# A new order of the start-up of chunked attention feeding a SoLU network, with some VectorE work given to GpSimd and two stores to SyncE

## The chip, the cores and the metric

The kernel runs on one core of a Trainium2 chip. A core has five engines with queues of their own: TensorE (PE) multiplies matrices, VectorE (DVE), ScalarE (ACT) and GpSimd (POOL) work elementwise, and SyncE (SP) issues transfers, which the core's 16 DMA engines carry out. The metric is the device time of one execution in microseconds (us); the time of a kernel is the median of several executions.

## The reference

Attention runs within chunks of 64 positions: 8 batches, 8 heads, 576 positions, head width 64. The heads are joined to 4608 rows of 512, and a network with a SoLU (h times softmax of h) and a normalization follows.

```python
scores = scale * np.matmul(q_c, k_c.transpose(0, 1, 2, 4, 3))
scores = scores - np.max(scores, axis=-1, keepdims=True)
attn = np.exp(scores)
attn = attn / (np.sum(attn, axis=-1, keepdims=True) + 1e-09)
out = np.matmul(attn, v_c)
...
h = x @ w_in                                  # 512 -> 1024
h_max = np.max(h, axis=-1, keepdims=True)
e = np.exp(h - h_max)
sm = e / (np.sum(e, axis=-1, keepdims=True) + 1e-09)
solu = h * sm
...
ln = (solu - mu) / np.sqrt(var + 1e-06) * g_ln
return (ln @ w_out).astype(np.float32)        # 1024 -> 512
```

## The kernel before, in words

The 4608 rows are cut into 36 tiles of 128 rows, two chunks each. For every tile the kernel turns q and k so that the head width lies on partitions, multiplies them to scores, takes the softmax, multiplies with v, multiplies the 512 columns with the first weight, applies SoLU and the normalization, turns the result z and multiplies it with the second weight. To keep accuracy each operand of the two large products is split into a high and a low part (x_h and x_l, wi_h and wi_l, z_h and z_l, wo_h and wo_l), and three of the four products of parts are added in PSUM: 24 products of 128x512 for each weight and tile.

The weights arrive as 64-bit numbers. Eight units of 1 MB (four of the first weight, four of the second) are loaded and put together from their two 32-bit words in steps.

The work falls into two parts. A loop over tiles 5 to 35 is the steady part. Ahead of it stands a start-up, written out as a list of words, START: each word calls one step of one tile or unit, and a word that comes again resumes a step that is in parts. Every engine takes its instructions in the order of this list, through a helper (the reason why nearly all instructions carry line 54). Only what is issued through `nc.scalar` directly is left to the scheduler, and that was the transfer of the first stores (line 630). A second list, MOVED, names steps that go to another engine than usual. The words, with what each part does and on which engine:

- `n:i`, `v:i`, `P:u`, `g`, `Q`/`q`: SP issues loads: q and k of tile i for turning on PE, v of tile i, weight unit u, the gain, a batch's q and k (32 transfers, eight for each `q:8`).
- `w:n`: n products of the identity with itself on PE, whose result nobody reads (the warm-up, line 717 on).
- `N:i:x`: four transpositions of q (x = 0) or k (x = 1) of tile i on PE; then their copy from PSUM on ACT, or on DVE if MOVED says so. `G`: the gain, turned.
- `S:i`: 32 small products for the scores. `A:i`: maximum and subtraction on DVE; then the exponential on ACT. `B:i`: sum, reciprocal and scaling on DVE (`softmax_b`). `T:i`: transposition of the probabilities on PE; then four copies on ACT. `U:i`: the same by a DVE transposition and, for odd i, eight transfers, four each from POOL and SP. `V:i`: 32 small products with v; x_h on ACT; x_l on DVE.
- `c:u`: clamp of unit u's upper words, on POOL; then a Prelu on ACT. `b:u`: the lower words, on DVE. `C:u`: the two joined, on DVE. `t:u`: high part, on ACT. `d:u`: low part, on DVE (`unit_low`).
- `M:i`: 24 products with the first weight (for tile 0 in four parts, one for each unit). `X:i`: row maximum on DVE; then the exponential on ACT. `Y:i`: a product and sum on DVE, the last reader of M's PSUM tile; then a linear step on ACT, or where MOVED puts it. `R:i`: the normalization's factor, on ACT and POOL.
- `z:i:x`: half x of z turned on PE; its copy z_h on ACT; z_l on DVE. `Z:i`: z turned on DVE and, for odd i, sixteen transfers, half from POOL, half from SP. `F`: a third of a tile's products with the second weight (eight). `o:i`: the result scaled on ACT and its store.
- `K:9`: q and k of tile 9 turned on DVE from batch 2's 32 loads.

There are two PSUM banks for transpositions, so a third group waits for the first one's copy. All tiles but tile 1 share one PSUM tile for M, so M of a tile waits for the first half of Y of the tile before. The first pass of the loop works on tile 5: it begins with M of tile 5, and eight microseconds later multiplies tile 2's z, which `Z:3` sent on its way, with the second weight.

Of the kernel before, what the change touches and what calls it, by code (L numbers as in the profile page):

```python
# [15 lines left out]


START = """
n:0 w:3 N:0:0 N:0:0 w:1 N:0:1 N:0:1 g w:1 S:0 A:0 G P:0 P:0 n:1 A:0 c:0 c:0 w:3 N:1:0 N:1:0 w:1
N:1:1 b:0 N:1:1 G P:1 w:1 S:1 B:0 v:0 C:0 A:1 t:0 T:0 T:0 c:1 c:1 w:4 V:0 V:0 P:2 b:1 c:2 n:2  # L20
d:0 P:3 A:1 n:3 w:6 N:2:0 w:1 N:2:1 C:1 V:0 B:1 t:1 c:2 T:1 N:2:0 b:2 N:2:1 T:1 d:1 S:2 n:4
M:0 M:0 C:2 t:2 c:3 c:3 v:1 A:2 A:2 b:3 d:2 C:3 N:3:0 N:3:1 N:3:1 M:0 N:3:0 S:3 N:4:0 B:2 N:4:1
t:3 N:4:0 A:3 P:5 d:3 c:5 N:4:1 A:3 T:2 T:2 S:4 V:1 M:0 P:4 n:5 B:3 T:3 V:1 V:1 M:1 X:0 X:0 T:3
A:4 A:4 b:4 v:2 N:5:1 c:4 n:6 P:7 c:5 N:5:0 c:4 Y:0 Y:0 n:7 N:5:1 V:2 b:5 v:3 B:4 N:5:0 V:2 b:7
C:4 z:0:1 P:6 v:5 N:6:0 X:1 v:4 C:5 N:6:0 S:5 Q:2 q:8 t:4 V:2 d:4 N:6:1 N:6:1 X:1 t:5 A:5 Y:1
M:2 z:0:1 z:0:1 X:2 A:5 R:0 z:0:0 z:0:0 q:8 N:7:1 q:8 c:6 S:6 Y:1 V:3 X:2 T:4 T:4 z:0:0 d:5 F
V:3 Y:2 Y:2 N:7:0 A:6 c:6 c:7 V:3 b:6 B:5 C:6 n:8 N:7:0 M:3 R:1 c:7 q:8 N:7:1 C:7 T:5 z:1:0 t:6
T:5 S:7 t:7 d:6 X:3 X:3 d:7 V:4 V:4 Y:3 Y:3 R:2 z:1:1 A:6 F F A:7 V:4 z:1:0 z:1:0 v:6 Z:2 A:7
M:4 F B:7 Z:3 o:0 V:5 z:1:1 z:1:1 B:6 F F v:7 X:4 N:8:0 X:4 U:6 U:7 V:5 Y:4 V:5 K:9 Y:4 N:8:0
R:4 R:3 N:8:1 N:8:1 o:1  # L30
"""
# [31 lines left out]
def chunk_attention_then_solu_ffn(  # L63
# [18 lines left out]
    G = S // 32  # L82
    NT = B * S // P
# [23 lines left out]
    def po():  # L107
# [26 lines left out]
    ident = const.tile([P, P], F32, name="ident")  # L134
# [93 lines left out]
    def unit_low(x):  # L228
        kind, m = UNITS[x]
        a, top = scaled.pop(x), tops.pop(x)  # L230
        if kind == "in":
            dve.tensor_tensor(
                out=paired(wi_l[:, m, :]),
                in0=a.rearrange("p h (a b x) -> p (h a) x b", b=P, x=2),
                in1=top.bitcast(F32), op=ALU.subtract,
            )
            return
        for y in range(2):
            dve.scalar_tensor_tensor(
                out=wo_l[:, 2 * m + y, :], in0=a[:, y],  # L240
                scalar=g_sb[:, 2 * m + y:2 * m + y + 1], in1=top[:, y].bitcast(F32),
                op0=ALU.mult, op1=ALU.subtract,
            )
# [132 lines left out]
    def softmax_b(i):  # L376
        e = st[i, "e"]
        ssum = small.tile([P, H], F32, name="s_sum")
        dve.tensor_reduce(out=ssum, in_=ES[i % 2], axis=AX.X, op=ALU.add)
        rinv = small.tile([P, H], F32, name="s_rinv")  # L380
        dve.reciprocal(out=rinv, in_=ssum)
        a = st[i, "e"] = work.tile([P, H, CH], F32, name="s_e") if i < PE_TURNED else e
        dve.tensor_tensor(
            out=a, in0=e, in1=rinv.unsqueeze(2).to_broadcast([P, H, CH]), op=ALU.mult,
        )

# [228 lines left out]
    def store(i):  # L615
        _, r = st.pop((i, "n"))
        o = work.tile([P, DM], F32, name="o_sb")
        sums = st.pop((i, "o"))
        for x, po in enumerate(sums):
            cols = slice(x * DM // len(sums), (x + 1) * DM // len(sums))  # L620
            act.activation(o[:, cols], po[:, cols], AF.Copy, scale=r)
            stores.append((out[i * P:(i + 1) * P, cols], o[:, cols]))
        if not order.on or i >= NT - 3:
            store_rest()

    stores = []

    def store_rest():
        for to, of in stores:
            (sync if order.on and len(stores) == 1 else nc.scalar).dma_start(to, of)  # L630
# [46 lines left out]
    def third():  # L677
        m, p = queue.pop(0)
        ffn_out(m, p, 3)
        if p == 2:  # L680
            store(m)

    def third_ahead():

        m, p = queue.pop(0)
        ffn_out(m, p, 3)
        if p == 1 and m + 1 < NT:
            whole(z_half(m + 1, 0))
        if p == 2:
            if m + 1 < NT:  # L690
                whole(z_half(m + 1, 1))
            store(m)
# [41 lines left out]
    begun = {}
# [15 lines left out]
    for i in range(first, NT):  # L750
# [99 lines left out]
```

## Time and profile before

| What | Value |
|---|---|
| median of 3 runs | 475.97 us (475.63 to 477.59) |
| the profiled execution | 477.95 us |
| its span, first to last instruction | 476.2 us |
| busy share of the span: PE, DVE, ACT, POOL | 98%, 79%, 54%, 31% |
| first product of the loop (M of tile 5) | 82.15 us after the span's start |

In the rows of the profile `out<-in` names the tiles that an instruction writes and reads: `ph` is M's PSUM tile, `po` F's, `sx` that of scores and values, `tp` the banks of transpositions, `h_nmax` is X's maximum, `z<-ph,z` Y's first half, `s_nmax` and `e<-sx` are A, `s_sum`, `s_rinv` and `e<-e,s_rinv` are B, `w_a` and `w_b` are units on their way, `nat` is q and k for turning, `q_st` and `k_st` a batch's q and k. Rows of a timeline give start, duration, engine, line, operation, tiles and, in brackets, the idle time before it and what ended it. An engine's successive rows overlap by some 0.08 us, so the time that a queue takes is read from start to start.

### The profile page before, as it was taken

To read this page: it belongs to the slowest core of one execution; us is meant where nothing else is said; L and a number is where in the kernel's file an instruction comes from. 1 tells how busy PE (TensorE), PEld (TensorE's weight loads), DVE (VectorE), ACT (ScalarE), POOL (GpSimd) and SP (SyncE) were. 2 spreads that over 40 slices of the span, in tenths; PEclk is the share of its full clock that TensorE was granted. 3 is DMA by queue.
4 is the path that set the end of the run, shared out by engine and by line. 5 is a ranking of instruction groups with operands and counts; after the bars stand their busy time and mean duration, and the time that the engine had idled before them with its cause. 6 is when DMAs were issued, how large, how long until landed. Compare 5 with 4: busy or idle time off the path is not lost.

```text
span 476.2 us, 11114 instructions
## 1 busy us (share of the span) xinstructions
PE 465.6 (98%) x4212; PEld 382.6 (80%) x4212; DVE 374.3 (79%) x520; ACT 256.5 (54%) x423; POOL 147.7 (31%) x298
## 2 busy tenths in 40 slices
PE   7899998999999999999999999999999999999997
PEld 5677786888888888888888888888888888888876
DVE  3999997798869887878787878797979797954441
ACT  2879982646444645454545455454555554545552
POOL 2212725150505050505050505032414141423330
PEclk9999999999999999999999999999999999999999
DMA  8999979758886878696358596949743435343221
GB/s 221 308 288 220 202 134 199 166 154 154 200 144 162 158 175 166 164 168 154 88 138 159 136 185 144 182 110 188 156 115 97 126 90 135 85 116 104 74 60 73
DMA packets 192924, 72.57 MB, mean 152 GB/s; under 512 B 177188, under 2 KB 177960, under 8 KB 191976
## 3 DMA queue, kind: packets, MB, share of 16 engines
q1 hardware_dynamic: 185768, 58.23, 55.4%
q0 software_dynamic: 6528, 12.86, 10.4%
q8 instruction: 33, 0.54, 0.5%
q10 hardware_dynamic: 576, 0.79, 0.5%
q14 instruction: 19, 0.16, 0.1%
HBM read 36.70 MB, written 9.44 MB: 97 GB/s over the span
## 4 chain that ended last, share of the span: by engine, by line
PE 85%; DMA 6%; SPq 3%; DVE 3%; ACT 1%; issue 1%; ACTq 0%
PE po L54 38%; PE ph L54 38%; PE tp L54 5%; PE sx L54 4%; SPq L54 3%; DMA nat<-in_k_dram 2%; DMA nat<-in_q_dram 2%; DMA z_t<-z_b 1%; DMA k_st<-in_k_dram 1%; DVE h_nmax L54 0%; DVE w_a L54 0%; DVE wo_l L54 0%; ACT attn_t L54 0%; ACT z L54 0%; ACT z_h L54 0%
## 5 line engine op out<-in xcount | busy, mean ns | idle before, releaser
L54 PE MATMUL ph<-wi_l,x_h 128*128 128x512 f32 x288 | 112.9, 392 | 1.9 <-DVE z L54 1.8
L54 PE MATMUL po<-wo_l,z_h 128*128 128x512 f32 (+1 forms) x288 | 113.3, 393 | 0.1
L54 ACT ACTIVATE z<-ph,h_nmax 128x1024 f32<-128x1024 f32 x36 | 40.2, 1117 | 134.6 <-DVE h_nmax L54 134.6
L54 PE MATMUL ph<-wi_h,x_h 128*128 128x512 f32 x288 | 112.1, 389 | 0.0
L54 PE MATMUL po<-wo_h,z_l 128*128 128x512 f32 (+1 forms) x288 | 111.9, 389 | 0.0
L54 PE MATMUL po<-wo_h,z_h 128*128 128x512 f32 (+1 forms) x288 | 111.4, 387 | 0.0
L54 POOL DMA_DIRECT2D z_t<-z_b x144 | 71.7, 505 | 28.7 <-DVE z_b L54 24.5
L54 PE MATMUL ph<-wi_h,x_l 128*128 128x512 f32 x288 | 78.1, 390 | 0.0
L54 POOL TENSOR_TENSOR u<-ssq,eps 128x1 f32<-128x1 f32 x36 | 7.1, 198 | 212.1 <-ACT sq L54 211.9
L54 DVE TENSOR_REDUCE h_nmax<-ph 128x1 f32<-128x1024 f32 x36 | 44.0, 1221 | 30.2 <-PE ph L54 30.2
L54 PEld LDWEIGHTS ph<-wi_l,x_h 128*128 128x128 f32 x288 | 54.1, 188 | 13.8 <-ACT x_h L54 2.2
L54 PEld LDWEIGHTS po<-wo_h,z_l 128*128 128x128 f32 x288 | 54.1, 188 | 12.1 <-DVE z_l L54 1.0
L54 PEld LDWEIGHTS po<-wo_l,z_h 128*128 128x128 f32 x288 | 54.1, 188 | 11.9 <-ACT z_h L54 0.5
L54 PEld LDWEIGHTS ph<-wi_h,x_l 128*128 128x128 f32 x288 | 53.9, 188 | 11.6 <-DVE x_l L54 0.4
L54 PEld LDWEIGHTS ph<-wi_h,x_h 128*128 128x128 f32 x288 | 54.1, 188 | 11.0
L54 PEld LDWEIGHTS po<-wo_h,z_h 128*128 128x128 f32 x288 | 54.1, 188 | 10.5
L54 DVE TENSOR_TENSOR z_l<-z_t,z_h 128x1024 fp32r<-128x1024 f32 (+1 forms) x37 | 42.0, 1136 | 25.3 <-ACT z_h L54 23.9
L54 DVE SCALAR_TENSOR_TENSOR z<-ph,z 128x1024 f32<-128x1024 f32 x36 | 43.9, 1219 | 13.3 <-ACT z L54 13.2
L54 ACT ACTIVATE z<-z,z_sum 128x1024 f32<-128x1024 f32 x33 | 38.1, 1154 | 23.0 <-DVE z L54 22.4
L54 DVE STREAM_TRANSPOSE z_b<-z 128x1024 f32<-128x1024 f32 x34 | 41.2, 1211 | 3.8 <-ACT z L54 3.1
L54 ACT CAST z_h<-z_t 128x1024 fp32r<-128x1024 f32 (+1 forms) x37 | 35.9, 970 | 8.6 <-PE po L54 6.5
L54 ACT ACTIVATE o_sb<-po,r 128x512 f32<-128x512 f32 (+1 forms) x36 | 24.2, 673 | 24.9 <-POOL r L54 18.6
(76 smaller groups left out, 598.6 us busy)
## 6 DMA issues: line engine op xcount, KB each, us to landing
out_dram<-o_sb SPq DMA_DIRECT2D x33, 256.0 KB, 2.5
v_sb<-in_v_dram SPq DMA_DIRECT2D x32, 256.0 KB, 4.4
z_t<-z_b POOLq DMA_DIRECT2D x128, 64.0 KB, 2.8
z_t<-z_b SPq DMA_DIRECT2D x128, 64.0 KB, 2.9
q_st<-in_q_dram SPq DMA_DIRECT2D x96, 72.0 KB, 3.1
k_st<-in_k_dram SPq DMA_DIRECT2D x96, 72.0 KB, 3.1
w_raw<-in_moe_w_out_dram SPq DMA_DIRECT2D x4, 1024.0 KB, 7.4
attn_t<-a_b POOLq DMA_DIRECT2D x60, 64.0 KB, 3.8
```

Of the source, the lines that this page charges most:

```text
L54: ins = make(*args, **kwargs)
```

## The change

- START has the same words in another order, except for the warm-up: 21 products become 9, and each is 512 columns wide instead of 256. Unit 1 is loaded first, ahead of q and k of tile 0. M:0 starts after N:3, S:3 and N:4:0, where it used to start after S:2. X:3 is followed by d:6, Z:2, d:7, A:7 and only then by Y:3; it was followed by d:7 and Y:3. K:9 stands ahead of Y:4 instead of behind it, and U:7 ahead of Z:3.
- MOVED gives to GpSimd the scalings of B:0 and B:2 to B:7 and the low words d:0, d:2 and d:3. It gives to DVE the copies N:3:0, N:5:0, z:1:0 and z:1:1 (before on ACT) and Y:4's linear step (ACT); N:0:0 and N:8:0 go from DVE to ACT, b:7 from GpSimd to DVE, the linear steps of Y:0 and Y:3 from GpSimd to ACT.
- The stores of tiles 0 and 1 used to be issued by `o` on ScalarE's queue, outside the order. Now `o` only notes them, and two new words, O:0 and O:1 near the end of the list, issue them from SP.

```diff
-R:4 R:3 N:8:1 N:8:1 o:1
+P:1 n:0 b:1 w:3 N:0:1 c:1 c:1 P:0 n:1 C:1 P:0 g N:0:1 t:1 N:0:0 N:0:0 c:0 P:2 w:2 S:0 N:1:1
+N:1:1 d:1 N:1:0 c:2 c:0 A:0 A:0 n:2 N:1:0 G c:2 G b:0 C:0 w:2 S:1 v:0 N:2:0 B:0 N:2:0 A:1 t:0
+A:1 n:3 N:2:1 N:2:1 b:2 T:0 T:0 w:1 S:2 C:2 d:0 N:3:0 A:2 A:2 B:1 w:1 V:0 N:3:0 P:3 c:3 N:3:1
+V:0 V:0 T:1 t:2 d:2 b:3 n:4 N:3:1 n:5 S:3 A:3 T:1 N:4:0 N:4:0 c:3 A:3 B:2 C:3 M:0 v:1 N:4:1
+N:4:1 M:0 t:3 v:2 P:5 P:4 d:3 B:3 N:5:0 N:5:0 N:5:1 V:1 V:1 c:5 T:2 n:6 M:0 T:2 M:0 V:1 N:5:1
+X:0 X:0 S:4 V:2 V:2 n:7 P:6 A:4 c:5 b:5 c:4 T:3 T:3 Y:0 v:3 V:2 C:5 b:4 M:1 A:4 Y:0 t:5 z:0:0
+z:0:0 B:4 N:6:0 M:2 R:0 X:1 c:4 z:0:0 d:5 X:1 C:4 N:6:0 P:7 t:4 N:6:1 Y:1 N:6:1 N:7:1 X:2 S:5
+c:6 c:7 V:3 c:6 N:7:1 V:3 d:4 Q:2 q:8 z:0:1 v:5 v:4 X:2 A:5 z:0:1 V:3 N:7:0 N:7:0 q:8 A:5 F c:7
+Y:1 Y:2 Y:2 S:6 T:4 T:4 M:3 b:7 z:0:1 B:5 b:6 T:5 A:6 z:1:0 A:6 C:6 C:7 X:3 R:2 S:7 V:4 t:6 t:7
+n:8 d:6 V:4 Z:2 d:7 T:5 A:7 X:3 Y:3 A:7 q:8 F F z:1:1 V:4 B:7 v:6 M:4 o:0 z:1:0 z:1:0 B:6 z:1:1
+q:8 z:1:1 Y:3 V:5 v:7 X:4 R:1 U:6 U:7 Z:3 V:5 V:5 F F X:4 K:9 Y:4 Y:4 N:8:1 F R:4 N:8:0 O:0
+N:8:0 N:8:1 o:1 R:3 O:1
...
-            dve.tensor_tensor(
+            (pool if f"d:{x}" in moved else dve).tensor_tensor(
                 out=paired(wi_l[:, m, :]),
...
-        dve.tensor_tensor(
+        (pool if f"B:{i}" in moved else dve).tensor_tensor(
             out=a, in0=e, in1=rinv.unsqueeze(2).to_broadcast([P, H, CH]), op=ALU.mult,
         )
...
-        if not order.on or i >= NT - 3:
+        if i >= NT - 3:
             store_rest()
...
+    def store_one(i):
+        sync.dma_start(*stores.pop(0))
...
-        m = ident.unsqueeze(1).to_broadcast([P, 2, P])
+        m = ident.unsqueeze(1).to_broadcast([P, 4, P])
```

The end of the old list, for comparison of the places named above:

```
A:4 A:4 b:4 v:2 N:5:1 c:4 n:6 P:7 c:5 N:5:0 c:4 Y:0 Y:0 n:7 N:5:1 V:2 b:5 v:3 B:4 N:5:0 V:2 b:7
C:4 z:0:1 P:6 v:5 N:6:0 X:1 v:4 C:5 N:6:0 S:5 Q:2 q:8 t:4 V:2 d:4 N:6:1 N:6:1 X:1 t:5 A:5 Y:1
M:2 z:0:1 z:0:1 X:2 A:5 R:0 z:0:0 z:0:0 q:8 N:7:1 q:8 c:6 S:6 Y:1 V:3 X:2 T:4 T:4 z:0:0 d:5 F
V:3 Y:2 Y:2 N:7:0 A:6 c:6 c:7 V:3 b:6 B:5 C:6 n:8 N:7:0 M:3 R:1 c:7 q:8 N:7:1 C:7 T:5 z:1:0 t:6
T:5 S:7 t:7 d:6 X:3 X:3 d:7 V:4 V:4 Y:3 Y:3 R:2 z:1:1 A:6 F F A:7 V:4 z:1:0 z:1:0 v:6 Z:2 A:7
M:4 F B:7 Z:3 o:0 V:5 z:1:1 z:1:1 B:6 F F v:7 X:4 N:8:0 X:4 U:6 U:7 V:5 Y:4 V:5 K:9 Y:4 N:8:0
R:4 R:3 N:8:1 N:8:1 o:1
```

More of the change, by code (lines that the diff above doesn't have):

```diff
@@ L18 @@
 START = """
[L19 to L29, printed above, removed]
-R:4 R:3 N:8:1 N:8:1 o:1
+P:1 n:0 b:1 w:3 N:0:1 c:1 c:1 P:0 n:1 C:1 P:0 g N:0:1 t:1 N:0:0 N:0:0 c:0 P:2 w:2 S:0 N:1:1
@@ L31 @@
+c:6 c:7 V:3 c:6 N:7:1 V:3 d:4 Q:2 q:8 z:0:1 v:5 v:4 X:2 A:5 z:0:1 V:3 N:7:0 N:7:0 q:8 A:5 F c:7
[3 more added lines that the diff above has]
+N:8:0 N:8:1 o:1 R:3 O:1
 """
 MOVED = """
-N:0:0=dve N:8:0=dve N:8:1=dve Y:0=pool Y:1=pool Y:3=pool b:7=pool c:0=pool c:1=pool c:2=pool
@@ L36 @@
-c:3=pool c:4=pool c:5=pool c:6=pool c:7=pool
+B:0=pool B:2=pool B:3=pool B:4=pool B:5=pool B:6=pool B:7=pool N:3:0=dve N:5:0=dve N:8:1=dve
+Y:1=pool Y:4=dve c:0=pool c:1=pool c:2=pool c:3=pool c:4=pool c:5=pool c:6=pool c:7=pool
+d:0=pool d:2=pool d:3=pool z:1:0=dve z:1:1=dve
 """
@@ L629, in store_rest @@
         for to, of in stores:
-            (sync if order.on and len(stores) == 1 else nc.scalar).dma_start(to, of)
+            (sync if len(stores) == 1 else nc.scalar).dma_start(to, of)
         stores.clear()
+    def store_one(i):
+        sync.dma_start(*stores.pop(0))
     NAT = -(-S // P)
@@ L721, in warm @@
             pe.matmul(
-                ph[:, 0, :2 * P].rearrange("p (x m) -> p x m", x=2), ident, m, start=True, stop=True
+                ph[:, 0, :].rearrange("p (x m) -> p x m", x=4), ident, m, start=True, stop=True
             )
@@ L730, in chunk_attention_then_solu_ffn @@
         "b": unit_bits, "C": unit_join, "t": unit_high, "d": unit_low, "M": ffn_in, "X": solu_a, "Y": solu_b,
-        "R": variance, "Z": z_turn, "z": z_half, "F": product, "o": store,
+        "R": variance, "Z": z_turn, "z": z_half, "F": product, "o": store, "O": store_one,
         "K": turn, "w": warm,
```

## The prediction

> **What bounds the kernel now.** I read the page's span first, then the busy time by stretch, with cuts where TensorE starts the products of row tiles 0, 2, 4 and 5 with the first weight (words M:0, M:2, M:4, and the first pass of the loop).
>
> ```profile
> span 476.2 us, 11114 instructions
> ```
>
> ```profile
> 0.00:23.36 23.36, 19.15 (x204) 14.58 (x205) 14.69 (x21) 13.14 (x20) 5.15 (x13) 1.00 0.93 264
> 23.36:44.41 21.05, 20.21 (x259) 16.06 (x253) 20.67 (x29) 17.00 (x30) 4.83 (x4) 1.00 1.04 253
> 44.41:67.24 22.83, 22.65 (x232) 18.43 (x230) 21.57 (x32) 21.73 (x43) 10.39 (x9) 1.00 0.89 184
> 67.24:82.15 14.91, 13.07 (x90) 10.12 (x88) 11.88 (x19) 4.66 (x10) 6.76 (x13) 1.00 0.99 186
> 82.15:476.20 394.05, 390.53 (x3440) 323.38 (x3440) 305.46 (x423) 200.00 (x324) 120.57 (x261) 1.00 0.61 137
> ```
>
> Columns: stretch, its length, then PE, weight loads, DVE, ACT, POOL busy, granted clock, DMA share, GB/s. From 82.15 on PE is busy 390.53 of 394.05 us, in code that the change leaves alone except for the place of two stores. So the change is worth what it moves the first product of the loop, now at 82.15. Call that point E. Ahead of it three things are nearly full at once: PE, DVE (20.67 of 21.05, 21.57 of 22.83) and the DMA engines (share 0.89 to 1.04). Relief on one of them only reaches the next.
>
> What ends last just ahead of E is in the chain of waits:
>
> ```profile
> 70.86 4.09 DMA k_st<-in_k_dram
> ...
> 75.03 0.41 ACTq L630
> ...
> 75.49 0.60 ACT z_h L54
> ...
> 76.11 0.69 DVE z_l L54
> ...
> 82.15 5.68 PE ph L54 x24
> ```
>
> The store of tile 0 (L630, on ScalarE's queue) waits for a k load, the copy z_h stands behind it, and DVE's z_l behind that. PE's own rows:
>
> ```profile
> 1.43 2.93 PE L54 MATMUL ph<-ident 128*128 128x256 f32 x6 [1.43 <-POOL e L357]
> ...
> 7.97 1.56 PE L54 MATMUL ph<-ident 128*128 128x256 f32 x6
> ...
> 49.08 1.07 PE L54 MATMUL ph<-wi_h,x_l 128*128 128x512 f32 x4
> ...
> 67.24 0.39 PE L54 MATMUL ph<-wi_l,x_h 128*128 128x512 f32 x1
> ...
> 72.71 0.39 PE L54 MATMUL po<-wo_l,z_h 128*128 128x512 f32 x1
> ...
> 79.27 1.04 PE L54 MATMUL tp<-ident,nat 128*128 128x128 f32 x8
> 82.15 0.47 PE L54 MATMUL ph<-wi_l,x_h 128*128 128x512 f32 x1 [1.84 <-DVE z L54]
> ...
> 90.19 0.50 PE L54 MATMUL po<-wo_l,z_h 128*128 128x512 f32 x1
> ```
>
> A tile's 24 products take 67.24 to 72.71, 5.47 us, so eight of them (a word F) 1.82; four transpositions (N, T, z) take half of 1.04, 0.52; I take 0.6 for the 32 small products of S or V. PE stands idle 1.84 us before E. So without the stall E comes at 80.3 at the earliest: 1.84 us, 0.4% of the span, is what moving the store can give in the old order of words. Under 0.5% is about what a measurement of this kernel can't tell from no change.
>
> **The change, step by step.** DVE's prices are best taken from start to start:
>
> ```profile
> 61.28 1.41 DVE L54 SCALAR_TENSOR_TENSOR wo_l<-w_a,g_sb,wo_h 128x512 fp32r<-128x512 f32 x2
> 62.60 1.22 DVE L54 TENSOR_REDUCE h_nmax<-ph 128x1 f32<-128x1024 f32 x1
> 63.78 1.41 DVE L54 SCALAR_TENSOR_TENSOR wo_l<-w_a,g_sb,wo_h 128x512 fp32r<-128x512 f32 x2
> ...
> 66.85 0.69 DVE L54 TENSOR_REDUCE s_nmax<-sx 128x8 f32<-128x512 f32 x1
> 67.58 0.69 DVE L54 TENSOR_TENSOR e<-sx,s_nmax 128x512 f32<-128x512 f32 x1
> 68.18 0.68 DVE L54 TENSOR_TENSOR x_l<-sx,x_h 128x512 fp32r<-128x512 f32 x1
> ...
> 69.38 1.24 DVE L54 STREAM_TRANSPOSE z_b<-z 128x1024 f32<-128x1024 f32 x1
> 70.54 0.65 DVE L54 TENSOR_REDUCE s_sum<-e 128x8 f32<-128x520 f32 x1
> ...
> 71.46 0.69 DVE L54 TENSOR_TENSOR e<-e,s_rinv 128x512 f32<-128x512 f32 x1
> 72.07 1.24 DVE L54 STREAM_TRANSPOSE z_b<-z 128x1024 f32<-128x1024 f32 x1
> ...
> 79.41 1.29 DVE L54 STREAM_TRANSPOSE a_b<-e 128x512 f32<-128x512 f32 x2
> 80.77 1.22 DVE L54 SCALAR_TENSOR_TENSOR z<-ph,z 128x1024 f32<-128x1024 f32 x1
> ...
> 82.52 0.70 DVE L54 STREAM_TRANSPOSE qT<-q_st 128x512 f32<-128x512 f32 x1
> ```
>
> That gives 1.32 for d of an output unit, 1.18 for X, 1.33 for A (66.85 to 68.18), 0.6 for x_l, sub of z, b or an eviction, all of 512 columns or at two a step (67.58 to 68.18), 1.16 for Z, 0.92 for the sum and reciprocal of B (70.54 to 71.46) and 0.61 for its scaling, 1.36 for U:6 and U:7 together, 1.2 for Y's first half (80.77's row), 1.2 for K:9 (twice 0.70, less the overlap); for C and d of an input unit, both over 1024 columns, I take X's 1.18.
>
> *Work moved.* DVE loses seven scalings (7 × 0.61 = 4.3) and three input units' low words (3 × 1.18 = 3.5), two evictions go and two come, and it gains b:7 (0.6), two evictions of z:1 (1.2) and the linear step Y:4 (bounded by 0.6 and 1.2). Net some 5 us less on DVE. This is off the path wherever DVE waits for PE.
>
> *Price on GpSimd.* No row has GpSimd on two wide inputs. Nearest are these, GpSimd's first and DVE's after them:
>
> ```profile
> 36.65 1.10 POOL L54 TENSOR_SCALAR w_a<-w_raw 128x1024 f32<-128x1024 f32 x1 [1.47 <-DMA w_raw<-in_moe_w_out_dram]
> 39.55 1.49 POOL L54 TENSOR_SCALAR z<-z,z_sum 128x1024 f32<-128x1024 f32 x1 [1.80 <-DVE z L54]
> 47.60 3.73 POOL L54 TENSOR_SCALAR w_b<-w_raw 128x1024 uint32<-128x1024 uint32 x1 [6.57 <-DVE s_nmax L54]
> ```
>
> ```profile
> 36.82 1.48 DVE L54 TENSOR_SCALAR w_b<-w_raw 128x1024 uint32<-128x1024 uint32 x1
> ```
>
> One input of 1024 columns takes 1.10, so a scaling of 512 lies between half of that, 0.55, and half of 3.73, 1.87. Two inputs at twice the one-input rate give 1.1, and 2.2 for a unit's low words; I take these. GpSimd gets 7 × 1.1 + 3 × 2.2 = 14.3 us and loses b:7 (3.73) and two linear steps (2.2), beside the 27 us that it is busy now ahead of E (5.15, 4.83, 10.39 and 6.76 of the stretches): no bound by itself. But the two engines get in each other's way: DVE's w_b began at 36.82 under GpSimd's w_a, which ended at 37.75, and took 1.48, so only 0.55 of it lies past that end; and GpSimd's z took 1.49 where w_a of the same size took 1.10. [...] Each moved operation can thus hand back to DVE between nothing and its own 1.1 or 2.2. Only those beside a DVE chain that sets PE's time count; there I take 0.5 in all, the overlap of B:5 with b:6, from 0 to 1.1.
>
> *Warm-up.* 21 products of 256 columns become 9 of 512. The first three cost 2.72 from 1.43 to the next row's start, later ones 0.52 each; twice that is 5.4 for the first three, then 1.04 each. They fill time in which PE waits for loads: unit 1 is now loaded ahead of tile 0's q and k, so the longer first group covers a later N:0. Taken as nothing.
>
> *To the end of M:2.* M:0 now stands behind N:3, S:3 and N:4:0, which PE used to do later (2.2 us). N:4:0 needs in all 6.5 MiB of loads (units 0 to 3, tiles 0 to 3 and half of 4, v:0), 6.8 MB. By 23.36 the trace had moved 0.264 × 23.36 = 6.2 MB; the rest at 253 GB/s takes 2.5, so 25.9, then N:4:0, its predecessors' evictions and M:0: I take 27.2 (26.4 if all is ready, 29 if the evictions queue on ACT behind unit 3's steps), against 23.36. From there to M:2 PE has M:0 and M:1 (10.9), seven groups of transpositions (3.6) and three of S or V (1.8): 16.3, and 0.5 for changes between them: M:2 at 44.0, its end at 49.5 to 49.8, against 50.15 now. The old list had also done N:6:1 and S:5 (1.1) by then. So the two orders are even here.
>
> *From the end of M:2 to M:4.* PE has three N, one of z and T:4 (2.6), S:5, S:6, V:3 (1.8), F (1.8), M:3 (5.5), then T:5 and z:1:0 (1.0), S:7 and V:4 (1.2), two F (3.6), z:1:1 (0.5): 18.0. DVE has in the new order X:2, d:4, A:5, x_l 3, Y:2 (5.6); b:7, a sub, B:5's sum, b:6, A:6, C:6, C:7 (6.4); X:3, d:6, Z:2, d:7, A:7, Y:3 (7.5): 19.5. M:4 writes the PSUM tile that Y:3 reads, so it waits for DVE: 49.7 + 19.5 + 0.2, and 0.5 of contention, M:4 at about 69.9, against 67.24. This is where the gain goes: X:3 waits for M:3, and four DVE steps stand between X:3 and Y:3 where the old list had one d.
>
> *From M:4 to E.* M:4 ends at 75.4. PE then has V:5, three F, two N, as now: 72.71 to the end of 79.27's row is 7.6, less 0.2 that the last one's pipeline hides: 7.4, so 82.8. DVE has X:4, U:6, U:7, Z:3, x_l 5, K:9, Y:4: 1.18 + 1.36 + 1.16 + 0.6 + 1.2 + 1.2 = 6.7, and 0.2: 82.3. The old stall behind the store is gone and DVE just fits beside PE, if K:9 does not wait.
>
> *K:9's wait.* K:9 reads batch 2's 32 loads of q and k. It used to stand behind Y:4; now Y:4 stands behind it.
>
> ```profile
> 70.13 6.02 SPq L54 DMA_DIRECT2D k_st<-in_k_dram x8
> ...
> 76.95 6.82 SPq L54 DMA_DIRECT2D z_t<-z_b x8
> ```
>
> ```profile
> L54 SPq DMA_DIRECT2D k_st<-in_k_dram x16: 443/496/1782, 64.1 to 75.6; - x16
> ...
> DMA to landing us min/median/max: 2.5/3.5/5.3
> ```
>
> The last two rows are the view of k_st: all 16 of its issues, shortest, median and longest, and their landing. SP issues its last one by 76.15, landed by 79.7 with the median and 81.4 with the longest. The new list has the same loads ahead, and v:6 as well (one issue more, 0.75). For E at 82.8 K:9 must start by 80.2. Landing at 79.0 to 81.5 thus costs 0 to 1.3; I take 0.
>
> *The stores and z_t.* O:0 and O:1 keep SP behind ACT's o:1, after U:7 and Z:3; nothing due early stands behind them. But SP now issues U:7's four copies (3.0 at k_st's 0.75 each) ahead of Z:3's eight (6.82). Z:3 leaves DVE some 3.2 us ahead of E (x_l 5, K:9, Y:4), U:7 4.3 ahead, so at these paces the last copy is issued 5.5 after E and lands 2.5 later; z_t's first user on PE comes 8.04 after E (90.19 less 82.15) and needs it split first, about 2.2. PE would wait 2. At 0.5 an issue, the median of k_st's 16, the last one is issued 1.7 after E and nothing waits. 0 to 2; I take 0.2, near the lower end, because SP's queue is empty by then.
>
> *Sum.* E goes from 82.15 to 82.8, and 0.2 come behind it: span 476.2 + 0.85 = 477.05. The profiled execution took 477.95, 1.75 over its span, so it would take 478.8; the median of the runs shown is 475.97, 1.98 below that execution, so the median becomes **476.8**.
>
> **The rivals.**
> *K:9 late (slower).* If the last k load lands past 80.2, E = landing + 2.6 (K:9, Y:4, 0.2). If the last eight start at 73 instead of 70.13, behind v:4, v:5 and v:6, take 6.02 for the issue and 5.3 to land, that is 84.3, E = 86.9 and the time 480.7. For it: DMA share 0.99 in the last stretch. Against: GpSimd's Z:3 copies no longer compete before that landing.
> *GpSimd in DVE's way (slower).* B:5, B:7 and B:6 stand beside DVE's 19.5 and 6.7; at 1.87 each and wholly in its way they add 5.6, half of it 2.8: E near 85.6, 479.4. It decides from 0.5 on, what I took. [...]
> *Only the store's stall goes (faster).* If DVE's four steps behind X:3 find time, because M:3 ends earlier than DVE's chain says or loads land without the pauses that they have now, PE alone sets E: 49.7 + 18.0 + 5.5 + 7.4 = 80.6, or 79.3 if M:0 starts at 26: 474.4 to 473.1. For it: 5 us less on DVE. Against: the sum of one queue in order, above.
> *Half clock (slower).* Ahead of M:0 PE has nine N, four S, two T, a V (9) and the warm-up (11.6), so it idles some 6.6 of its first 27.2 us, where the first stretch now leaves 4.2. In the trace the first six rows run at 0.45 each and later ones at 0.26. If it fell back to the first pace for half of M:0, 2.7 us of products take 4.7: 2.0 more, 478.6. [...]
> *The change doesn't do what it says.* Every step has its queue in the list, and the stores now have one too; under 0.01, and counted with the forecast.
>
> **How the numbers follow.** Forecast, E between 81.4 and 84.4 (475.4 to 478.4 with the 0.2): 0.62. PE alone sets E: 0.16, of which 0.09 goes under 473.6. K:9 late: 0.10. GpSimd: 0.08. Half clock: 0.04. The 0.5% bounds are 473.6 and 478.4. Faster: those 0.09 and 0.01 of the forecast's tail, 0.1. Slower: 0.08 of K:9, 0.06 of GpSimd, 0.03 of the clock, 0.17. The range takes in the faster rival down to 473.8 and the slower ones up to 479.4, and leaves 0.2 out.
>
> **What would show it.** Right: M:2 starts near 44; M:4 starts near 69.9, PE idle 1.5 to 2.5 us before it for DVE's z; PE idle little before E; ACT no longer idle for k loads near 75; GpSimd's scalings at 1.1 and low words at 2.2. Wrong: M:4 within 0.3 of PE's own pace, PE waiting on nat loads for more than 2 us between M:0 and M:1, E off by more than 1.5, or a change after E.

## The result, and the profile after

| | kernel before | changed kernel |
|---|---|---|
| median of its runs | 476.78 us (474.86 to 478.68, 6 runs) | 482.65 us (481.14 to 485.25, 6 runs) |
| the profiled execution, and its span | 477.95, 476.2 us | 481.58, 479.8 us |

The ratio is 1.0125 with a 95% interval of 1.0083 to 1.0167: 5.9 us slower, where 476.8 us in a range from 473.8 to 479.4 had been predicted. The profiled executions lie 3.6 apart only, because that of before is above its median and that of after below. Of the changed kernel's runs those granted a clock of 1.000 took 481.14 and 481.58 us, those at 0.992 and 0.993 took 484.88 and 485.25; the two between, at 0.995 and 0.999, took 482.12 and 483.19.

The busy time by stretch, cut at the first products of M:0, M:2, M:4 and E as in the prediction (stretch, length, PE, weight loads, DVE, ACT, POOL, clock, DMA share, GB/s):

```profile
0.00:29.23 29.23, 20.49 (x224) 11.47 (x225) 16.26 (x24) 16.28 (x26) 9.88 (x16) 1.00 1.04 251
29.23:46.72 17.49, 16.74 (x175) 13.45 (x174) 11.54 (x18) 12.64 (x22) 10.12 (x7) 1.00 1.00 281
46.72:72.58 25.86, 24.22 (x268) 19.26 (x266) 25.27 (x38) 23.35 (x45) 8.72 (x9) 1.00 0.89 172
72.58:85.31 12.73, 12.73 (x89) 10.30 (x89) 11.55 (x19) 4.44 (x9) 6.65 (x12) 1.00 0.68 129
85.31:479.80 394.49, 390.80 (x3443) 323.46 (x3440) 303.44 (x420) 199.50 (x323) 121.73 (x263) 1.00 0.61 137
```

E comes 3.16 us later than before (85.31 against 82.15), and 0.44 more is lost behind it. The late start is there at M:0 already: 29.23 against 23.36. PE idles 8.7 us of the first stretch, where it idled 4.2 of a shorter one. From M:2 on the stretches are near what was predicted: PE's one long wait is for Y:3 (1.11, the row at 72.58), and PE is never idle from M:4 to E.

```profile
28.85 0.63 PE L55 MATMUL tp<-ident,nat 128*128 128x128 f32 x4 [1.71 <-DMA nat<-in_q_dram]
29.23 0.48 PE L55 MATMUL ph<-wi_l,x_h 128*128 128x512 f32 x1
...
36.55 0.50 PE L55 MATMUL ph<-wi_l,x_h 128*128 128x512 f32 x1 [0.20 <-POOL wi_l L55]
...
72.58 0.50 PE L55 MATMUL ph<-wi_l,x_h 128*128 128x512 f32 x1 [1.11 <-DVE z L55]
```

Two things hold M:0. Its first part stands behind N:4:0, which waits for tile 4's q. Its last part needs unit 3's low words, and waits for them in spite of the late start. What unit 3 waited for is in the chain of waits (start, duration, what):

```profile
12.31 3.70 SPq L55
...
18.25 9.35 DMA w_raw<-in_moe_w_in_dram
...
27.75 1.53 POOL w_a L55
...
29.29 1.25 POOL wi_l L55
...
31.65 2.04 POOL s_e L55
...
34.07 2.44 POOL wi_l L55
...
36.55 1.65 PE ph L55 x6
```

The chain names one transfer and then GpSimd: the clamp, part of another unit's low words, a scaling, unit 3's low words. But the chain follows an engine's own queue where the waits are short, and the low words did not wait for the scaling, which ended at 33.69: their row (at 34.07, further down) has 0.38 of idle time that ScalarE's high part ended. ScalarE's rows give the other path:

```profile
29.57 0.59 ACT L55 COPY qT<-tp 128x512 f32<-128x512 f32 x1 [1.67 <-PE tp L55]
30.05 1.06 ACT L55 ACTIVATE w_a<-w_a 128x1024 f32<-128x1024 f32 x1
...
32.82 1.17 ACT L55 CAST wi_h<-w_a 128x1024 fp32r<-128x1024 f32 x1 [0.71 <-DVE w_a L55]
```

Unit 3's clamp ended at 29.28, its Prelu began at 30.05, behind the copy of N:4's q, which waited for PE; then come the join on DVE, the high part on ScalarE and the low words on GpSimd. The two paths end within 0.38 us of each other, so that is the most which a shorter path on ScalarE alone could gain, and a shorter queue on GpSimd alone gains nothing. In the trace of before, SP and GpSimd have for the same unit

```profile
14.06 4.85 SPq L54 DMA_DIRECT2D w_raw<-in_moe_w_in_dram  x1
```

```profile
24.14 1.13 POOL L54 TENSOR_SCALAR w_a<-w_raw 128x1024 f32<-128x1024 f32 x1 [4.62 <-DMA w_raw<-in_moe_w_in_dram]
```

so unit 3 has landed 3.6 us later in the new list, where tile 3's q and k are loaded ahead of it instead of behind. GpSimd's prices are near those taken, except under DVE's join:

```profile
17.55 1.04 POOL L55 TENSOR_TENSOR s_e<-e,s_rinv 128x512 f32<-128x512 f32 x1
...
31.65 2.04 POOL L55 TENSOR_TENSOR s_e<-e,s_rinv 128x512 f32<-128x512 f32 x1
34.07 2.42 POOL L55 TENSOR_TENSOR wi_l<-w_a,wi_h 128x1024 fp32r<-128x1024 f32 x1 [0.38 <-ACT wi_h L55]
```

```profile
31.15 1.64 DVE L55 SCALAR_TENSOR_TENSOR w_a<-w_a,w_b 128x1024 uint32<-128x1024 uint32 x1 [0.67 <-ACT w_a L55]
```

The scaling that began at 31.65, under DVE's join of two inputs (1.64, where the prediction takes 1.18 for it), took 2.04 instead of 1.04. The one at 17.55 took 1.04 beside DVE operations that read scores from PSUM. The join ended at 32.79 and the scaling 0.9 after that, so most of a scaling's 1.04 lies behind the join's end; by what the two hold each other up no row shows.

### The profile page after: what moved, and what is told of

Read it like the earlier page. It is cut to its first block, busy times and chain, and to the rows that moved or that the text cites. A ratio compares the mean times of both kernels' runs of the same rounds, so it can differ in the third digit from the quotient of the medians.

```text
span 479.8 us, 11071 instructions
## 1 busy us (share of the span) xinstructions
PE 465.0 (97%) x4188; PEld 377.9 (79%) x4188; DVE 368.0 (77%) x514; ACT 256.2 (53%) x422; POOL 157.1 (33%) x305
## 4 chain that ended last, share of the span: by engine, by line
PE 83%; DVE 5%; SPq 4%; DMA 3%; issue 2%; POOL 2%; ACT 1%; DVEq 0%; ACTq 0%; POOLq 0%
PE ph L55 38%; PE po L55 38%; SPq L55 4%; PE sx L55 4%; PE tp L55 4%; DMA w_raw<-in_moe_w_in_dram 2%; POOL wi_l L55 1%; DVE h_nmax L55 1%; DMA z_t<-z_b 1%; DVE wo_l L55 1%; DVE z L55 1%; DVE z_b L55 1%; DVE w_a L55 0%; DVE e L55 0%; POOL s_e L55 0%
## 5 line engine op out<-in xcount | busy, mean ns | idle before, releaser
L55 ACT ACTIVATE z<-z,z_sum 128x1024 f32<-128x1024 f32 x34 | 39.3, 1155 | 22.5 <-DVE z L55 21.9
L55 ACT ACTIVATE sq<-z 128x1024 bf16<-128x1024 f32 x36 | 37.5, 1043 | 4.5 <-DVE z L55 4.5
```

Of the source, the lines that this page charges most:

```text
L55: ins = make(*args, **kwargs)
```

## The experiments

Each ratio is against runs of the kernel before taken beside it, with its 95% interval; E, M:0, M:2 and M:4 are the starts of those products in the run's own trace.

**The parts of the change.** First the stores alone, in the old list:

```diff
-R:4 R:3 N:8:1 N:8:1 o:1
+R:4 R:3 N:8:1 N:8:1 O:0 o:1 O:1
```

> The old list and old engines; only the stores of tiles 0 and 1 go to SyncE, at the end of the list. If the stall behind the first store was worth what the rows say, PE's 1.84 us of idle time before the loop goes, the loop's first product comes at 80.3 to 80.6 instead of 82.15, and the kernel is 1.5 to 1.9 us (0.3 to 0.4%) faster than before. If another wait takes its place (DVE's chain up to Y:4, or loads), no change within 0.5 us.

Measured: 475.35 us, ratio 0.9974 (0.9957 to 0.999), E at 80.44, with no wait ahead of it:

```profile
79.65 1.03 PE L54 MATMUL tp<-ident,nat 128*128 128x128 f32 x8
80.44 0.48 PE L54 MATMUL ph<-wi_l,x_h 128*128 128x512 f32 x1
```

The stall is what the prediction read it as (80.3 without it), and this part alone is faster than both kernels. Next GpSimd's ten operations alone, in the old list:

```diff
+B:0=pool B:2=pool B:3=pool B:4=pool B:5=pool B:6=pool B:7=pool d:0=pool d:2=pool d:3=pool
```

> The old list; only the seven scalings of probabilities and the three low words go to GpSimd. If the new order is what costs, this is within 1 us of before, and the loop starts at 81 to 83. If GpSimd is what costs (its 1 us for a scaling and 2.4 us for low words in chains that PE waits for, and blocked turns beside DVE), this alone is 2 to 4 us slower than before.

Measured: 481.76 us, 1.0108 (1.0089 to 1.0127), E at 86.27. Rows of DVE, POOL, ACT and PE, and two stretches:

```profile
21.17 1.22 DVE L53 TENSOR_TENSOR wi_l<-w_a,wi_h 128x1024 fp32r<-128x1024 f32 x1
```

```profile
22.48 1.09 POOL L53 TENSOR_SCALAR w_a<-w_raw 128x1024 f32<-128x1024 f32 x1 [6.98 <-DVE wi_l L53]
23.53 2.40 POOL L53 TENSOR_TENSOR wi_l<-w_a,wi_h 128x1024 fp32r<-128x1024 f32 x1
```

```profile
23.60 1.06 ACT L53 ACTIVATE w_a<-w_a 128x1024 f32<-128x1024 f32 x1 [3.94 <-POOL w_a L53]
24.56 0.57 ACT L53 COPY qT<-tp 128x512 f32<-128x512 f32 x1
```

```profile
25.18 1.11 PE L53 MATMUL tp<-ident,s_e 128*128 128x128 f32 x4 [3.08 <-ACT qT L53]
```

```profile
20.00:25.00 5.00, 1.66 (x10) 1.11 (x10) 2.70 (x4) 1.40 (x2) 2.52 (x2) 1.00 1.09 309
25.00:30.00 5.00, 4.82 (x46) 3.88 (x47) 4.00 (x4) 4.18 (x9) 3.80 (x3) 0.66 1.30 206
```

Not GpSimd's busy time costs here: it stood idle for 6.98 us ahead of the clamp of unit 2 (the row at 22.48). What ended that wait was DVE's low words of unit 1, at 22.39. The moved operation, unit 0's low words, comes behind the clamp in GpSimd's queue (23.53). In the kernel before DVE had made them from 16.02 on, and the clamp of unit 2 began at 17.98, on the landing of its load. `w_a`, which a clamp writes and low words are the last to read, has two buffers (pool `work`); so the likely reading is that the move took away the buffer that used to come free first. It rests on these rows and the kernel's text; no run adds a buffer. The rest is shown by the rows: ACT's Prelu waits for the clamp, tile 2's copies stand behind the Prelu, and PE waits for the copies. Behind that idle of 3.08 us the granted clock is 0.66 over five microseconds. Then the reverse, the changed kernel with the ten operations back on DVE:

```diff
-B:0=pool B:2=pool B:3=pool B:4=pool B:5=pool B:6=pool B:7=pool d:0=pool d:2=pool d:3=pool
```

> The changed kernel with the same seven scalings and three low words back on DVE. If the order is what costs, the time stays within 1.5 us of the changed kernel (481 to 484), and the product of row tile 0 with unit 3 still starts after 35. If GpSimd is what costs, that product starts by 34, the loop by 83, and the time falls to 478 or less.

Measured: 489.21 us, 1.0261 (1.0235 to 1.0287), E at 90.64, with one wait of

```profile
37.20 0.66 PE L53 MATMUL tp<-ident,s_e 128*128 128x128 f32 x4 [3.11 <-DVE qT L53]
```

That is outside both ranges that were expected. So list and engines cannot be priced apart: the moves cost 5 us in the old list and save 6.6 in the new one.

**The clock.** The changed kernel with 17 wide warm-up products instead of 9, in the same places and two new ones ahead of T:1 and N:4:0:

```diff
-V:0 V:0 T:1 t:2 d:2 b:3 n:4 N:3:1 n:5 S:3 A:3 T:1 N:4:0 N:4:0
+V:0 V:0 w:1 T:1 t:2 d:2 b:3 n:4 N:3:1 n:5 S:3 A:3 T:1 w:2 N:4:0 N:4:0
```

> The changed kernel with 17 warm-up products of 512 columns instead of 9, the added ones where PE idled in the first 29 us. If the clock is the cause of what the median shows beyond the profiled run (the granted clock was 0.992 to 0.999 in four of the changed kernel's six runs, and those four were the longest), the clock is 1.0 in every run and the median falls by about 2 us, to 480 to 481. If the clock doesn't matter, the median stays at 482 to 483, or rises by what the added products delay.

Measured: 482.57 us, 1.0127 (1.0107 to 1.0146), clock 0.999 or 1.000 in all five runs, which lie within 1.1 us, but E at 86.38, because the products last past the load that they fill:

```profile
28.13 1.98 PE L55 MATMUL ph<-ident 128*128 128x512 f32 x4
29.95 0.60 PE L55 MATMUL tp<-ident,nat 128*128 128x128 f32 x4
```

They buy the steady clock with as much delay. The other way round, the kernel before with 9 of its 21 products (an excerpt; of the nine places five go, three keep two products each and the first keeps its three):

```diff
-N:0:0 w:1 N:0:1 N:0:1 g w:1 S:0 ... n:3 w:6 N:2:0 w:1 N:2:1
+N:0:0 N:0:1 N:0:1 g S:0 ... n:3 w:2 N:2:0 N:2:1
```

> The kernel before with 9 warm-up products of 256 columns in place of 21, nothing else changed. If the warm-up only fills time in which TensorE waits, E (first product of the loop) stays at 82.2 (81.9 to 82.5) and the time at 476.7. If idle time on TensorE lowers its clock, as in the rows of the run with only the GpSimd moves (clock 0.58 for 4 us after an idle of 3.08), some stretch of this run between 0 and 30 us shows a clock under 0.9, products there stand 0.4 apart instead of 0.23, E comes 1 to 2.5 us later and the time is 477.7 to 479.2.

Measured: 478.06 us, 1.0035 (1.0013 to 1.0057). Between 0 and 50 us the profiled run (clock 0.999) shows 1.00 throughout and M:0 2 us *earlier* (21.36), and E at 81.40; ten of the twelve runs were granted 0.989 to 0.996. But the lower ones among these are not the longer ones (476.92 us at 0.989, 480.71 at 0.993, 478.06 at 1.000). So neither expectation holds whole: less filling starts M:0 sooner, lowers the clock in most runs, and costs 0.35%, which the clock alone does not explain. In the profiled run PE still waits for Y:4 ahead of E (1.88), and the lead is lost behind E, in part in these two waits:

```profile
137.54 0.62 PE L54 MATMUL tp<-kT,qT 64*64 64x64 f32 x26 [0.27 <-DVE kT L54]
...
140.04 0.50 PE L54 MATMUL po<-wo_h,z_l 128*128 128x512 f32 x1 [0.69 <-DVE z_l L54]
```

**Y:3.** The changed kernel with X:3 and Y:3 ahead of A:7:

```diff
-n:8 d:6 V:4 Z:2 d:7 T:5 A:7 X:3 Y:3 A:7 q:8
+n:8 d:6 V:4 Z:2 d:7 T:5 X:3 Y:3 A:7 A:7 q:8
```

> The changed kernel with X:3 and Y:3 ahead of A:7's first half, nothing else changed. Step (M:2 to M:4) of the prediction: M:4 waits for Y:3 at the end of DVE's queue, 1.1 us of idle in the trace of the changed kernel. If so, M:4 comes 1.1 earlier after M:3 and E at about 84.2, the time near 481.5. The rival is that TensorE's own sequence or the next wait (z of tile 1, K:9) is as late: E 85.0 to 85.4, the time 482.6.

Measured: 481.67 us, 1.0115 (1.0074 to 1.0155). PE's wait ahead of M:4 falls from 1.11 to 0.23, as expected; the interval does not tell this kernel from the changed one. Its profiled execution was one with a clock of 0.993, and so shows what the changed front can do, since nothing ahead of M:3 differs:

```profile
25.00:30.00 5.00, 2.64 (x41) 2.22 (x42) 3.44 (x7) 2.99 (x7) 2.09 (x2) 0.78 0.97 153
30.00:35.00 5.00, 5.00 (x16) 3.99 (x15) 2.85 (x5) 3.56 (x5) 3.82 (x3) 0.54 1.03 265
```

```profile
28.71 1.08 PE L55 MATMUL tp<-ident,nat 128*128 128x128 f32 x4 [1.53 <-DMA nat<-in_q_dram]
29.45 0.78 PE L55 MATMUL ph<-wi_l,x_h 128*128 128x512 f32 x1
30.02 0.63 PE L55 MATMUL ph<-wi_h,x_h 128*128 128x512 f32 x1
30.45 0.63 PE L55 MATMUL ph<-wi_h,x_l 128*128 128x512 f32 x1
...
73.66 0.50 PE L55 MATMUL ph<-wi_l,x_h 128*128 128x512 f32 x1 [0.23 <-DVE z L55]
```

PE was busy 2.64 us of the five ahead of 30; the changed kernel's trace has 2.50 there and a clock of 1.00. Here the clock fell, M:0's products stood 0.43 apart (30.02 to 30.45), and M:2 came at 48.48 instead of 46.72: up to M:2 the half clock costs 1.8 us in this execution. The changed kernel's own runs at 0.992 and 0.993 took some 3.7 us longer than those at 1.000; how much of that is lost behind M:2 no trace shows. Nor does any show why it strikes some runs and not others: ahead of this fall no single wait is longer than 1.53 us (the row at 28.71), ahead of the fall to 0.66 above there is one of 3.08, and the changed kernel's own trace has one of 1.71 with the clock at 1.00 behind it.

**Inside the front.** M:0's first two parts ahead of N:4:

```diff
-T:1 N:4:0 N:4:0 c:3 A:3 B:2 C:3 M:0 v:1 N:4:1 N:4:1 M:0 t:3
+T:1 M:0 M:0 N:4:0 N:4:0 c:3 A:3 B:2 C:3 v:1 N:4:1 N:4:1 t:3
```

> The changed kernel with M:0's first two parts ahead of N:4 (they stood between N:4's two groups and behind them), nothing else changed. Theory one: the 1.71 us that TensorE waits for q of tile 4 in front of M:0 is what the new place of M:0 costs; then M:0 starts at 27.1 instead of 29.2, M:2 at 45.0, E at 83.6 and the time is 480.9. Theory two: M:0's last part waits for unit 3's low words, which GpSimd ends at 36.5; then M:0 starts at 27.1 too, but the fourth part still near 36.5, M:2 near 46.7, E near 85.3 and the time 482.6.

Measured: 484.17 us, 1.0177 (1.0134 to 1.0219). M:0 started at 27.42 and M:2 at 47.48, which is theory two. ACT's rows, and PE's:

```profile
30.97 0.59 ACT L55 COPY qT<-tp 128x512 f32<-128x512 f32 x1 [2.71 <-PE tp L55]
31.45 1.06 ACT L55 ACTIVATE w_a<-w_a 128x1024 f32<-128x1024 f32 x1
```

```profile
37.49 0.50 PE L55 MATMUL ph<-wi_l,x_h 128*128 128x512 f32 x1 [0.15 <-POOL wi_l L55]
```

Unit 3's Prelu now stood behind the copy of N:4, which waited for PE. Hence the next, with the Prelu ahead as well:

```diff
+T:1 c:3 M:0 M:0 N:4:0 N:4:0 A:3 B:2 C:3 v:1 N:4:1 N:4:1 t:3
```

(The word's first part, the clamp, stands further ahead, so this one is the Prelu.)

> As the run with M:0 ahead of N:4 (M:0 at 27.4, M:2 at 47.5, E at 86.2), and with the clamp and the Prelu of unit 3 ahead of M:0 and N:4, nothing else. In that run ScalarE's Prelu of unit 3 began at 31.45, though GpSimd's clamp had ended at 27.3, because the copy of N:4's q stood ahead of it in ScalarE's queue and waited for TensorE (idle 2.71). Theory (unit 3's chain through the queues sets M:0's last part): the Prelu starts near 28.4, the low words end near 34.0 instead of 37.4, M:2 starts at 44.3 to 45.3, E comes at 83.0 to 84.0, the time is 480.4 to 481.4. Rival (what the front lacks is loads and GpSimd time, not the order of queues): M:2 at 46.5 or later, E from 85.2 on, the time 482.6 or more.

Measured: 481.92 us, 1.0112 (1.0095 to 1.013); the Prelu began at 28.25, M:0's last part at 36.09 still behind GpSimd's low words, M:2 at 46.08, E at 84.82. Against the run before that is 1.4 earlier, as the theory has it, but not the 2.2 to 3.2 expected; against the changed kernel 0.5. The queue was one link of several: GpSimd stood idle for 1.23 us ahead of the low words (33.60), because ScalarE's high part began at 32.37, behind N:4's copies, though the join had ended at 31.48. With M:0 ahead of N:4, unit 3 loaded ahead of tile 3's q and k, and its low words on DVE (without the earlier Prelu):

```diff
-A:1 n:3 N:2:1 ... N:3:0 P:3 c:3 N:3:1
+A:1 P:3 n:3 N:2:1 ... N:3:0 c:3 N:3:1
...
-d:0=pool d:2=pool d:3=pool
+d:0=pool d:2=pool
```

> As the run before, and with unit 3's load ahead of tile 3's q and k and unit 3's low words on DVE instead of GpSimd. Theory two (unit 3 late): unit 3 lands 2 to 3 us earlier (24.6 to 25.6 instead of 27.6), M:0's fourth part no longer waits, M:2 starts at 44.0 to 45.0, E at 82.6 to 83.6, the time is 480.0 to 481.0. Theory one alone (only the wait for tile 4): no better than the run before. A third possibility: tile 3's q and k come later by as much, TensorE waits for N:3 instead, and E stays at 85.0 to 85.6.

Measured: 490.43 us, 1.029 (1.0252 to 1.0328). The third possibility, and worse than put (E at 91.75):

```profile
24.38 0.63 PE L55 MATMUL tp<-ident,nat 128*128 128x128 f32 x4 [2.35 <-DMA nat<-in_q_dram]
...
39.70 0.63 PE L55 MATMUL tp<-ident,s_e 128*128 128x128 f32 x4 [2.89 <-DVE qT L55]
```

PE waits for tile 3 instead, and then for a copy that stands behind unit 3's steps on DVE. Last, the changed kernel with tile 5's load behind N:4:

```diff
-b:3 n:4 N:3:1 n:5 S:3 A:3 T:1 N:4:0 N:4:0 c:3 A:3 B:2 C:3 M:0 v:1 N:4:1 N:4:1 M:0
+b:3 n:4 N:3:1 S:3 A:3 T:1 N:4:0 N:4:0 c:3 A:3 B:2 C:3 M:0 v:1 N:4:1 N:4:1 n:5 M:0
```

> The changed kernel with the load of tile 5's q and k behind N:4 instead of in front of S:3, nothing else. Theory one (transfers in flight share the DMA engines, so what is issued behind unit 3 and tile 4 delays them): unit 3 lands at 26.6 to 27.1 instead of 27.6, N:4's first group starts at 27.5 to 28.3 instead of 28.85, E at 84.4 to 85.0, the time 481.8 to 482.3. Theory two (they land in the order of their issue): N:4 at 28.85 as before and N:5 later, E at 85.3 to 86.5, the time 482.6 to 483.8.

Measured: 483.28 us, 1.0144 (1.0121 to 1.0166), N:4 at 28.74, 0.1 earlier: this load, issued behind tile 4's, did not delay it. Then Prelu and Y:3 together:

```diff
+T:1 c:3 M:0 M:0 N:4:0 N:4:0 A:3 B:2 C:3 v:1 N:4:1 N:4:1 t:3
...
+n:8 d:6 V:4 Z:2 d:7 T:5 X:3 Y:3 A:7 A:7 q:8
```

> As the run with unit 3's Prelu ahead, and with X:3 and Y:3 ahead of A:7. If the loss in front of M:2 and the wait for Y:3 are independent terms, it is another 0.9 to 1.1 us faster than that run (M:4 waits 0.2 instead of 1.1): E at 82.0 to 83.0, the time 479.4 to 480.4, still 3 above the kernel before. If they overlap, it equals that run.

Measured: 482.0 us, 1.0119 (1.0089 to 1.0148): M:4's wait fell to 0.26, but the profiled execution lost 3 us to a late load near 20 us, and the time cannot be told from either part.

**Front against tail.** The old list up to M:2, then the changed one, with the engines of each:

```diff
+Y:1 z:0:0 z:0:0 M:2 R:0 z:0:0 d:5 N:7:1 X:2 c:6 c:7 V:3 c:6 N:7:1 V:3 X:2 z:0:1 V:3 N:7:0 N:7:0
```

> The old list with its engines and its narrow warm-up up to M:2, and from M:2 on the changed list with its engines and its two stores on SP. Where the loss lies: the landmarks of the single traces put 2.3 us of it in front of M:2 and 0.85 between M:2 and E. If so, M:2 starts at 43.7 to 44.5 as in the old list, E comes at 81.9 to 83.1 (1.1 less where it was done already, S:5 and N:6:1), and the time is 476.2 to 477.6. Rival: the loss is made behind M:2, by GpSimd's scalings or by Y:3, and the late front only hides it; then E comes at 84 to 85.5 and the time is 479 or more. Third: with the early front DVE's shorter list lets TensorE set E, at 80 to 81.5, and the time is 474.5 to 476.

Measured: 483.18 us, 1.0137 (1.0112 to 1.0161). This one told nothing, because of its seam: ACT reached unit 6's Prelu before the unit had landed, PE waited 3.33 us at 54.71, and the clock fell to 0.50 behind it. With c:6 and c:7 just ahead of M:3 instead:

```diff
+Y:1 Y:2 Y:2 S:6 T:4 T:4 c:6 c:7 c:6 c:7 M:3
```

> As the run with the old list up to M:2 and the changed one after it, with the clamps and Prelus of units 6 and 7 just ahead of M:3. In that run they stood where unit 6 had not landed yet, ScalarE waited 4.97 us for it, TensorE 3.33 at 54.71, and the clock fell to 0.50 behind that. If the loss lies in front of M:2, then without this seam M:2 is at 43.7 to 44.6, M:4 at 68.7 to 70.4 (25.9 behind M:2, less the S:5 and N:6 that were done already), E at 81.4 to 83.1 and the time is 476 to 477.6. If the tail of the changed list makes the loss by itself, M:4 comes at 71 or later, E at 84 or later and the time is 478.5 or more.

Measured: 478.35 us, 1.0034 (1.0015 to 1.0054), clock 0.999 or 1.000 in all 12 runs. The busy time by stretch, cut as above:

```profile
0.00:22.25 22.25, 20.10 (x204) 14.99 (x205) 13.95 (x21) 12.92 (x20) 5.05 (x13) 1.00 1.02 286
22.25:44.84 22.59, 21.01 (x262) 16.57 (x257) 22.28 (x30) 18.79 (x34) 5.00 (x4) 1.00 0.96 256
44.84:68.53 23.69, 22.50 (x227) 17.92 (x225) 22.05 (x33) 20.25 (x40) 10.48 (x9) 1.00 1.13 181
68.53:81.24 12.71, 12.71 (x88) 10.29 (x89) 11.55 (x19) 4.45 (x9) 6.65 (x12) 1.00 0.86 151
```

E comes at 81.24, 4.07 earlier than in the changed kernel, with the same tail and the same wait for Y:3 ahead of M:4 (1.08). M:2 is 1.9 of that earlier (44.84 against 46.72); the rest is mostly work that the old list has already done there, S:5 and N:6:1 among it: from M:2 to M:4 PE is busy 22.50 instead of 24.22. This run shows where the loss lies: of the 1.25% that the change costs, 0.91% (4.3 us of 476.7) goes when the old front is put back. With the order, the old front also brings back the old engines, the old warm-up and the steady clock, so it shows the place and not the share of each. From the stores alone (0.9974) to this kernel the new tail costs 0.60%, 2.9 us.

**What an earlier E is worth.** The old list with both stores on SP and three warm-up products fewer:

```diff
-c:1 c:1 w:4 V:0 ... n:3 w:6 N:2:0
+c:1 c:1 w:3 V:0 ... n:3 w:4 N:2:0
```

> The old list with the two stores issued by SP (475.35, E 80.44, M:0 at 22.75) and three of its 21 warm-up products fewer (two in front of N:2, one in front of V:0). Theory one (warm-up products that end after their successor is ready hold TensorE up): M:0 at 21.7 to 22.3, E at 79.3 to 80.0, the time 474.2 to 474.9, if the clock stays at 1.00. Theory two (they only fill waits, or the clock falls for want of them): E at 80.4 or later, the time 475.3 to 477.

Measured: 476.17 us, 0.9992 (0.9971 to 1.0013). E came at 79.20. M:0 did not come earlier (23.41, against 22.75 with the stores alone), so the lead, which shows first at M:4 (66.63 against 67.86), does not come from an earlier start. Behind E it went again:

```profile
86.97 1.02 PE L54 MATMUL sx<-attn_t,v_sb 64*64 64x64 f32 x29 [1.44 <-DMA attn_t<-a_b]
```

U:7's copies had not landed. With U:6 and U:7 ahead of X:4 in this list:

```diff
-F F v:7 X:4 N:8:0 X:4 U:6 U:7 V:5
+F F v:7 U:6 U:7 X:4 N:8:0 X:4 V:5
```

> The old list with both stores on SP, three warm-up products fewer, and U:6 and U:7 ahead of X:4. With three fewer alone E came at 79.2, but 1.44 us were given back at 86.97, where TensorE waited for U:7's copies. If those copies are what the earlier E runs into, they now land 1.2 us earlier, the wait falls to 0.3 or less and the time is 474.6 to 475.4, below both kernels. If another wait takes its place (X:4 later, so Y:4 and E later), E is 80.2 or later and the time 475.4 to 476.5.

Measured: 476.31 us, 0.9984 (0.9961 to 1.0006). That wait is gone, but DVE is later with Y:4, E is back at 80.82 and PE waits 0.53 ahead of it. The stores alone keep the lowest ratio of the study, though the intervals of these last two overlap theirs.

## Why the prediction was wrong, step by step

- *The stall behind the store:* right. Without it E is at 80.44, where 80.3 was put.
- *To the end of M:2:* this is the step that failed. It had M:0 at 27.2 and M:2 at 44.0 and called the two orders even; they came at 29.23 and 46.72. M:0 is late for N:4's load. The bytes were right (by 25.9 the changed kernel had moved 6.80 MB, as put), but the transfer asked for landed near 28.8: bytes moved by a time do not say which transfer is complete. And the bound put beside it, 29 "if the evictions queue on ACT behind unit 3's steps", had the right neighbour the wrong way round: unit 3's Prelu queues behind N:4's copy, and the list also loads unit 3 later; its chain ends at 36.5, so M:0's end was fixed even where its start was not. From M:0 to M:2 PE took 17.49, where 16.8 was put.
- *From the end of M:2 to M:4, and to E:* right. M:2 to M:4 took 25.86 against 25.9, PE waits 1.11 for Y:3 (less than the 1.5 to 2.5 put; the run with Y:3 earlier shows the cause), and M:4 to E took 12.73 against 12.9, with K:9 not late.
- *z_t:* PE waited 0.23 for z_l behind E, as put (0.2); SP issued the eight copies in 5.00 us, 0.62 each, between the two paces that gave 0 and 2. But the rest behind E, taken as a fixed 394.05, is not: it was 395.4 with E at 79.20, by the copies of U:7, and 395.9 with fewer warm-up products.
- *GpSimd's prices:* near (1.04 and 2.4 for 1.1 and 2.2), but for the 2.04 under the join. "No bound by itself" was right of its sum, and left out the order: in the old list the move alone held a clamp up for 6.98 us, and in the new one GpSimd's own steps are 4.0 of the 8.9 us from unit 3's landing to M:0's last part (the clamp 1.53, which was GpSimd's before too, and the low words 2.44, for which DVE takes 1.22).
- *The half clock:* given 0.04, with 1.00 in every stretch of the trace of before. Its size was near for the way to M:2 (2.0 put, 1.8 measured in one execution). But that trace has PE busy 19.15 of the 23.36 us ahead of M:0, where the step's own sum had 6.6 us of idle in 27.2, and in the five us from 25 of the execution whose clock fell PE was busy 2.64.
- *Scale:* of the 5.85 us between 482.65 and 476.8, 2.8 are the sum's, made against one execution (481.58 for 478.8). The other 3.05 are the way from there to the median: 1.98 was taken off, as for the kernel before, but the profiled execution of the changed kernel lies 1.07 below its median.

What stays open: no edit inside the new front brought back more than 0.5 us of E, so the front's loss is shown for the whole front (its order with its engines), and its division between tile 4's load, unit 3's load, ScalarE's queue and GpSimd's is argued from rows and chains of waits only. Of the 3.0 us that remain with the new tail (478.35 against 475.35 with the stores alone), the profiled executions show 0.8 up to E and 0.9 behind it; the other 1.2 is where these two executions lie to their medians. What makes the two terms is not split further.

## What to carry to other kernels

When an order is rewritten by hand, follow each step that a product needs through every queue it passes, from the issue of its load on: a sum of one engine's work is a bound only if the last input is there. An operation moved to another engine also moves the time at which its buffers come free, which is the likely reading of GpSimd's wait of 6.98 us in the old list. Take the parts of a change apart before judging it; here two words at the end of a list were worth 0.26% and lay under a loss of 1.5% (0.9974 to 1.0125). And read a clock of 1.00 only for the load at which it was recorded: here, with PE busy about half of the five us from 25, one execution kept 1.00 (2.50 busy), and another (2.64) fell to 0.54 in the next five and lost 1.8 us up to M:2. Where a change leaves the matrix engine that idle, price such a loss in.

## What the runs showed of the hardware that was not expected

- In the run with Y:3 earlier the clock fell to half (0.50 from 28 to 34 us, 0.54 as the mean of the five us from 30) without any single idle longer than 1.53 us, PE being busy 2.64 of the five before; at 2.50 of five the changed kernel's execution kept 1.00. At the lower clock M:0's products stood 0.43 us apart instead of 0.23.
- A GpSimd scaling of 128x512 took 1.04 or 1.05 us in five of the changed kernel's seven, 1.29 in the one at 61.03, and 2.04 in the one that began under DVE's join (1.99 under the join in the run with the earlier Prelu, again 0.9 past the join's end).
- The load of one megabyte of weights took 9.35 us from issue to landing in the changed front (DMA share 1.04 up to M:0); the longest of the kernel before took 9.9.
